# w_down in a decode block's feed-forward stage: two half transfers become one of four rows per partition, and its products move ahead of the gates

## The chip, the cores and the metric

The kernel runs on one core of one Trainium2 chip. The metric is the device time of one execution in microseconds. Before the change the median of three runs is 599.42 us (598.52 to 600.30).

## What is computed

The reference is one transformer block for a single token (batch 1, one row of D = 1024), its output and the gradients with respect to ten of its inputs: eleven outputs, the first of them the block's own. The block modulates a layer norm by a condition vector `c`, attends to the last 4096 of 65536 cached keys and values (32 query heads, 4 key heads), and then runs a gated feed-forward part:

```
h   = layernorm(x) * (1 + cb) + sb
g   = h @ w_gate          # (1024, 3584)
u   = h @ w_up            # (1024, 3584)
hh  = sigmoid(g) * u
ffn = hh @ w_down         # (3584, 1024)
x   = x + gb * ffn
```

The feed-forward part's gradients that matter here are, with `dffn = grad_out * gb` a row of 1024:

- d(w_down) = hh (outer product) dffn, 3584 x 1024;
- dhh = w_down @ dffn, a vector of 3584;
- du = dhh * sigmoid(g), dg = dhh * hh * (1 - sigmoid(g)), together `dug`;
- d(w_gate) and d(w_up) = h (outer product) dg and du;
- dh = w_gate @ dg + w_up @ du.

The gradients of the two caches have the caches' full shape, 65536 rows for each of 4 heads. All rows outside the window of 4096 are zero, and the kernel has to write them: this is the largest part of its traffic.

## The kernel before, in words

The kernel is one program with an order written out by hand. Each engine runs its own instructions in that order, and waits where an operand or a buffer isn't ready. DMAs are issued from two queues: SP (SyncE) and POOL (GpSimd). All of them are carried by the same 16 DMA engines. In the profile the SP queue's packets are q1 and POOL's are q0. Each queue's issuing engine is in order: an issue that waits holds all behind it.

**Fills.** The zero rows are written by 1 MB DMAs of a tile `zeros`, issued by `zero(n)` (line 169 in the profile) on POOL. How many stand at which place is fixed by lists at the top of the file (`Z_N`, `Z_B`, `Z_FOLD`, `Z_FFN`, `Z_END`). They serve as filler that keeps the DMA engines at work beside the loads and stores. In the feed-forward loop five blocks have three of them each, `(1, 0, 0, 2)`, the sixth has five and the last has four.

**Feed-forward stage.** F = 3584 is cut into NB = 7 blocks q of 512. For each block:

- w_gate and w_up arrive as 8 tiles j of 128 rows, in a double buffer `ug_v` (index q % 2). `load_ug(q, j0, 4)` issues two 512 KB loads, `store_ug` two 512 KB stores of the gradients, which take the place of the weights in the same buffer. Both are on POOL.
- w_down arrives in `wd_v`, one buffer of 8 KB per partition for all blocks, as two halves s of 256 rows. A half has two rows per partition. `load_wd(q, s)` and `store_wd(q, s)` are on SP. The gradient of w_down overwrites the weights in place, so the load of block q+1 has to wait until the store of block q has landed.
- `front(q)` (line 954, PE): 64 small products of `ug_v` with h2, giving g and u in PSUM. Which of the 512 features lies in which partition and column is set by w_down's row layout: feature 256*(i//2) + 2*p + i%2 stands in partition p, column i. PE reads `ug_v` with a step of 2 for this.
- `gates(q)` (lines 959 and 960, ACT): two sigmoids. `hh_ops(q)` (DVE): hh in bf16 and in f32, and hh*(1-sigmoid).
- `ffn_mm(q, s)` (line 971, PE): 16 products of a half of w_down with hh.
- `wd_ttr(q, s)` (DVE, the helper `ttr` at line 210, writes into `junk`): two multiply-and-sum instructions over 1024 columns, dhh = w_down . dffn. `b1k` is dffn broadcast to all partitions.
- `wd_outer(q, s)` (DVE, the helper at line 206): two outer products that overwrite the half of w_down by its gradient, then `store_wd`.
- `dug_part(q)`: two small DVE products, 8 PE transposes (line 990) and one ACT copy (line 991) that broadcast dug into `dug_b`, 1024 columns.
- The loop over j = 0..7: `ttr` of the tile with `dug_b` (DVE, line 210, in place), then an outer product into the tile, on ACT for j < 5 (line 241) and on DVE for the rest. Gate and up tiles 0 to 3 are stored after j = 3, 4 to 7 after j = 7.

`side()` takes one unit of unrelated work from a list: eight PE transposes (line 837) and an ACT copy (line 838).

For block q+1 the order before is: front, gates, one side unit, hh_ops, ffn_mm and two ttr of the first half, load of half the gate and up tiles of block q+2, two outer products and the store of the first half, side unit, the same for the second half with dug_part ahead of its outer products, the second half of the gate and up loads, the fills, and both w_down loads of block q+2.

After this stage come further gradients (attention, the projections, the modulation), and large stores to the end.

The functions that the diff touches:

Of the kernel before, what the change touches and what calls it, by code (L numbers as in the profile page):

```python
# [22 lines left out]
FB = 512  # L23
NB = F // FB
# [34 lines left out]
def kernel(  # L59
# [26 lines left out]
    nc = tc.nc  # L86
# [13 lines left out]
    def ar(off, size):  # L100
        return arena[:, int(off * KIB):int((off + size) * KIB)]
# [86 lines left out]
    def new_tp(name="tp"):  # L188
        p, tag = next_pool()
        return p.tile([P, 1024], BF16, name=name, tag=tag)  # L190
# [4 lines left out]
    def mulv(out, a, b):  # L195
        return tt(out, a, b, ALU.mult)

    def addv(out, a, b):
        return tt(out, a, b, ALU.add)

    def cp(out, a):
        return nc.vector.tensor_copy(out=out, in_=a)  # L202
# [6 lines left out]
    def ttr(out, w, b, acc):  # L209
        return nc.vector.tensor_tensor_reduce(out=out, in0=w, in1=b, scale=1.0, scalar=0.0,  # L210
                                              op0=ALU.mult, op1=ALU.add, accum_out=acc)
# [31 lines left out]
    def outer_dve(out, col, b):  # L243
        return ts(out, b, col, ALU.mult)
# [96 lines left out]
    def mod_tiles(ps, tiles, ts_, first, last=KD - 1):  # L341
        for t in ts_:
            for k in range(KD):
                nc.tensor.matmul(ps[:, k:k + 1], lhsT=tiles[t][:, k * P:(k + 1) * P],
                                 rhs=cs_bf[:, t:t + 1], start=(first and t == ts_[0] and k == 0), stop=(t == last),
                                 skip_group_check=True)
# [98 lines left out]
    def side(n=1):  # L445
        for _ in range(n):
            if jobs:
                jobs.pop(0)()
# [61 lines left out]
    for tb in range(4):  # L510
# [3 lines left out]
        tp = new_tp("tp_pT")  # L514
# [111 lines left out]
    for g in range(G):  # L626
        nbank = bank_pair("n_ps", g)
        for t_ in range(KT):
            s = g * KT + t_
# [52 lines left out]
    def bch(n=1):  # L682
        for _ in range(n):
            if not bq:
                return
            p, i, u = bq.pop(0)
            if i == 0:
                bbank[p] = bank_pair("b_ps", p)
            for a in range(4):
                h = 4 * u + a  # L690
                for k in range(2):
                    mm = nc.tensor.matmul(bbank[p][k][:, :], lhsT=a4[:, p, h, :], rhs=wo_t[u][:, a, k * 512:(k + 1) * 512],  # L692
                                          start=(i == 0 and a == 0), stop=(i == 7 and a == 3))
            zero(Z_B[nbq - 1 - len(bq)], recent(mm, 3))
            if i == 7:
                for k in range(2):
                    o = B_t[p][:, k * 512:(k + 1) * 512]
                    if k == 0 or p == NBP - 1:
                        nc.scalar.copy(out=o, in_=bbank[p][k][:, :])
                    else:  # L700
                        cp(o, bbank[p][k][:, :])
# [81 lines left out]
    def park(p, pl, tag):  # L783
        BT_ps[p] = pl.tile([P, D], BF16, name="BT_ps", tag=tag)
        for i in range(KD):
            nc.tensor.transpose(BT_ps[p][:, i * P:(i + 1) * P], B_t[p][:, i * P:(i + 1) * P], ident_bf[:, :])
# [58 lines left out]
    ug_v = arena[:, 16 * KIB:48 * KIB].rearrange("p (h q j k f) -> p q h j k f", h=2, q=2, j=4, k=2)  # L845
    wd_v = ar(152, 8).rearrange("p (i d) -> p i d", i=4)

    def wd_dram(t, q, s):
        return t[q * FB + s * 256:q * FB + s * 256 + 256, :].rearrange("(p j) d -> p j d", j=2)

    def load_wd(q, s):
        nc.sync.dma_start(out=wd_v[:, 2 * s:2 * s + 2, :], in_=wd_dram(B_w_down, q, s))

    def store_wd(q, s):
        nc.sync.dma_start(out=wd_dram(out_8, q, s), in_=wd_v[:, 2 * s:2 * s + 2, :])

    def ug_part(view, q, j0, n):
        return view[:, j0:j0 + n, q * FB:(q + 1) * FB]
# [8 lines left out]
    def store_ug(q, j0, n):  # L867
        for k, view in ((0, dwu_view), (1, dwg_view)):
            nc.gpsimd.dma_start(out=ug_part(view, q, j0, n), in_=ug_tile(q, k, j0, n))  # L869
# [23 lines left out]
    load_ug(0, 4, 4)  # L893
    park(2, pna, "na")
    park(3, pna, "na")
    load_wd(0, 0)
    bch(2)
    tr_unit(B_t[6], ar(56, 2))()
    cp(scr, B_t[4])
    B_t[4] = scr  # L900
    load_wd(0, 1)
    mod_tiles(md_ps, sb_t, range(4, 8), False)
    cp(sb_, md_ps[:, 0:KD])
    mulv(h2, ln2, cb1)
# [32 lines left out]
    dug_b = scr  # L937
# [10 lines left out]
    def front(q):  # L948
        gu = gu_t[q % 2]
        for col, k in ((4, 0), (0, 1)):  # L950
            for i in range(4):
                f0 = 256 * (i // 2) + i % 2
                for j in range(KD):
                    nc.tensor.matmul(gu[:, col + i:col + i + 1], lhsT=ug_v[:, q % 2, j // 4, j % 4, k, f0:f0 + 255:2],  # L954
                                     rhs=h2_bf[:, j:j + 1], start=(j == 0), stop=(j == KD - 1))

    def gates(q):
        r, gu = small[q % 2], gu_t[q % 2]
        nc.scalar.activation(out=r["sg"], in_=gu[:, 0:4], func=ACT.Sigmoid)
        nc.scalar.activation(out=r["om"], in_=gu[:, 0:4], func=ACT.Sigmoid, scale=-1.0)  # L960

    def hh_ops(q):
        r, up = small[q % 2], gu_t[q % 2][:, 4:8]
        mulv(r["hh_bf"], r["sg"], up)
        mulv(r["hh"], r["sg"], up)
        mulv(r["hom"], r["hh"], r["om"])

    def ffn_mm(q, s):
        for i in (2 * s, 2 * s + 1):
            for k in range(KD):  # L970
                nc.tensor.matmul(ffn_ps[:, k:k + 1], lhsT=wd_v[:, i, k * P:(k + 1) * P],
                                 rhs=small[q % 2]["hh_bf"][:, i:i + 1], start=(i == 0 and k == 0),
                                 stop=(i == 3), skip_group_check=True)

    def wd_ttr(q, s):
        for i in (2 * s, 2 * s + 1):
            ttr(junk, wd_v[:, i, :], b1k, small[q % 2]["dhh"][:, i:i + 1])

    def wd_outer(q, s):
        for i in (2 * s, 2 * s + 1):  # L980
            outer_dve(wd_v[:, i, :], small[q % 2]["hh"][:, i:i + 1], b1k)
        store_wd(q, s)

    def dug_part(q):
        r = small[q % 2]
        mulv(r["dug_bf"][:, 0:4], r["dhh"], r["sg"])
        mulv(r["dug_bf"][:, 4:8], r["dhh"], r["hom"])
        tp = new_tp("tp_dug")
        for i in range(8):
            nc.tensor.transpose(tp[:, i * P:(i + 1) * P], r["dug_bf"][:, i:i + 1].broadcast_to([P, P]), ident_bf[:, :])  # L990
        nc.scalar.copy(out=dug_b.rearrange("p (s f j) -> p s f j", s=4, j=2),  # L991
                       in_=tp.rearrange("p (s j f) -> p s f j", s=4, j=2))

    jobs.append(tr_unit(B_t[7]))
    for h in range(HQ):
# [3 lines left out]
    def unpark(p):  # L999
        nc.scalar.copy(out=B_home[p], in_=BT_ps[p][:, :])  # L1000

    front(0)
    gates(0)
    hh_ops(0)
    ffn_mm(0, 0)
    wd_ttr(0, 0)
    side(2)
    wd_outer(0, 0)
    ffn_mm(0, 1)
    wd_ttr(0, 1)  # L1010
    side(1)
    dug_part(0)
    wd_outer(0, 1)
    zero(Z_FOLD[2])
    load_wd(1, 0)
    load_wd(1, 1)
    for q in range(NB):
        z = Z_FFN[q]
        more = q + 1 < NB
        for j in range(KD):  # L1020
            w = ug_v[:, q % 2, j // 4, j % 4, :, :].rearrange("p k f -> p (k f)")
            ttr(w, w, dug_b, dh2acc[:, q * KD + j:q * KD + j + 1])
            if not more and j in (3, 5, 6):
                unpark({3: 2, 5: 0, 6: 4}[j])
            (outer_act if j < 5 else outer_dve)(w, h2[:, j:j + 1], dug_b)
            if more and 0 < j < 5:
                side()
            if j == 0:
                if q == 0:
                    cp(ffn, ffn_ps)  # L1030
                else:
                    addv(ffn, ffn, ffn_ps)
            if j == 3:
                store_ug(q, 0, 4)
                zero(z[0])
        store_ug(q, 4, 4)
        zero(z[1])
        if more:
            front(q + 1)
            gates(q + 1)  # L1040
            side()
            hh_ops(q + 1)
            ffn_mm(q + 1, 0)
            wd_ttr(q + 1, 0)
            if q + 2 < NB:
                load_ug(q + 2, 0, 4)
            wd_outer(q + 1, 0)
            zero(z[2])
            side()
            ffn_mm(q + 1, 1)  # L1050
            wd_ttr(q + 1, 1)
            side()
            dug_part(q + 1)
            wd_outer(q + 1, 1)
            if q + 2 < NB:
                load_ug(q + 2, 4, 4)
            zero(z[3])
            if q + 2 < NB:
                load_wd(q + 2, 0)
                load_wd(q + 2, 1)  # L1060
        else:
            zero(z[2] + z[3])
    assert not jobs
# [269 lines left out]
```

## Time and profile before

| | |
|---|---|
| median of 3 runs | 599.42 us |
| the profiled execution, time | 598.03 us |
| its span | 596.2 us |
| PE, DVE, ACT, POOL busy | 69%, 57%, 45%, 27% of the span |
| moved by DMA | 246.63 MB, mean 414 GB/s |
| software queue (POOL) | 217.60 MB, packets took 95.1% of 16 engines |
| hardware queue (SP) | 28.32 MB, 13.1% |
| feed-forward stage, first block's loop to the last block's loop | 324.4 to 464.0 us of the span |
| DMA rate in that stage | 407 GB/s |

The span is the time from the first to the last record of the profile. Rows of a chain or a timeline give the start in us from the span's start, the duration in us, and then the instruction: engine, line, tile. A row `DMA out_dram<-arena` in the chain is the time from a DMA's issue until what waited for its landing could go on. In a timeline, what stands in square brackets is how long the engine was idle before, and what ended it. The queue shares can sum to over 100%, as packets of the two queues overlap on an engine. The clock that was granted to PE in the feed-forward stage is 0.50.

### The profile page before, as it was taken

What the parts mean: (1) busy time and instruction counts of PE and PEld (TensorE: products, weight loads), DVE (VectorE), ACT (ScalarE), POOL (GpSimd) and SP (SyncE); (2) the same over time, 40 slices, a digit from 0 to 9 for tenths busy, and PEclk for the clock granted to TensorE, in tenths of its full rate; (3) what the DMA queues carried; (4) which work ended last, traced back from release to release, by engine and by line L of the source; (5) the groups of instructions that cost most, each with busy time, mean ns of one, the idle gap of its engine ahead of it and who ended that gap; (6) DMA issues with size and microseconds to landing.
All of it is one profiled execution on the core that took longest, in us unless ns stands there. A gap on an engine that the chain in (4) does not pass through costs nothing.

```text
span 596.2 us, 11043 instructions
## 1 busy us (share of the span) xinstructions
PE 409.2 (69%) x4587; PEld 275.6 (46%) x4612; DVE 337.7 (57%) x641; ACT 266.0 (45%) x408; POOL 159.4 (27%) x253
## 2 busy tenths in 40 slices
PE   3997688999999989999975436445445086774220
PEld 3995334334344545546654425434334066574220
DVE  3654499999511010070007587896787887858360
ACT  2589514567211014212224565773765835883110
POOL 3113123222222122222222224433423263223100
PEclk9999699999999999999995555555555586855555
DMA  8999999999999999999999999999999999999997
GB/s 348 421 417 420 413 425 417 426 425 424 429 420 424 421 430 422 423 423 423 422 399 412 420 387 414 404 405 409 403 410 408 420 420 413 422 423 426 424 426 326
DMA packets 45026, 246.63 MB, mean 414 GB/s; under 512 B 5085, under 2 KB 5085, under 8 KB 24544
## 3 DMA queue, kind: packets, MB, share of 16 engines
q0 software_dynamic: 37536, 217.60, 95.1%
q1 hardware_dynamic: 7392, 28.32, 13.1%
q8 instruction: 36, 0.59, 0.4%
q14 instruction: 14, 0.11, 0.0%
q10 hardware_dynamic: 48, 0.01, 0.0%
HBM read 60.30 MB, written 185.60 MB: 412 GB/s over the span
## 4 chain that ended last, share of the span: by engine, by line
DMA 38%; PE 32%; DVE 16%; ACT 5%; issue 4%; POOL 0%; DVEq 0%; ACTq 0%; POOLq 0%; SPq 0%
DMA out_dram<-arena 18%; PE b_ps L692 10%; DMA out_dram<-zeros 9%; PE n_ps L637 6%; DMA arena<-in_B_w_gate_dram 6%; DVE arena L206 5%; DMA arena<-in_B_w_down_dram 4%; DVE arena L193 4%; DVE junk L210 2%; PE t_ps L599 2%; DVE arena L210 2%; PE tp_wq L454 2%; PE w_ps L395 2%; PE tp_side L837 1%; PE tp_k L435 1%
## 5 line engine op out<-in xcount | busy, mean ns | idle before, releaser
L692 PE MATMUL b_ps<-arena 128*128 128x512 bf16 x494 | 113.4, 379 | 1.0 <-issue 0.2
L169 POOL DMA_DIRECT2D out_dram<-zeros x114 | 62.3, 548 | 178.7 <-DMA out_dram<-zeros 57.4
L837 PE MATMUL tp_side<-ident_bf,arena 128*128 128x128 bf16 x432 | 51.7, 300 | 48.1 <-ACT arena L838 41.2
L193 DVE TENSOR_TENSOR arena<-arena 128x2048 bf16<-128x2048 bf16 x64 | 76.5, 1223 | 2.3 <-PE n_ps L637 0.3
L692 PEld LDWEIGHTS <-arena 128*128 128x128 bf16 x512 | 48.7, 98 | 55.9 <-issue 2.9
L838 ACT COPY arena<-tp_side 128x1024 bf16<-128x1024 bf16 x54 | 54.0, 1012 | 42.7 <-PE tp_side L837 41.8
L210 DVE CUSTOM_DVE_ANT_0 arena<-arena,scr 128x1024 bf16<-128x1024 bf16 x56 | 66.2, 1220 | 9.9 <-ACT scr L991 9.9
L637 PE MATMUL n_ps<-arena 128*128 128x512 bf16 x249 | 65.1, 378 | 6.9 <-DVE arena L193 5.0
L837 PEld LDWEIGHTS <-arena 128*128 128x128 bf16 x432 | 43.4, 139 | 53.0 <-issue 52.6
L241 ACT ACTIVATE arena<-scr,h 128x1024 bf16<-128x1024 bf16 x35 | 40.1, 1149 | 9.6 <-DVE dh2acc L210 7.8
L637 PEld LDWEIGHTS <-arena 128*128 128x128 bf16 x256 | 24.6, 97 | 41.6 <-issue 16.2
L1162 ACT ACTIVATE arena<-ps_kv 128x512 bf16<-128x512 f32 x48 | 26.1, 680 | 30.4 <-PE ps_kv L1158 30.0
L202 DVE CAST arena<-b_ps 128x512 bf16<-128x512 f32 x6 | 4.2, 692 | 61.6 <-PE b_ps L692 61.6
L210 DVE CUSTOM_DVE_ANT_0 junk<-arena,b1k 128x1024 bf16<-128x1024 bf16 x28 | 34.2, 1222 | 6.8 <-DMA arena<-in_B_w_down_dram 6.3
L1158 PE MATMUL ps_kv<-junk,arena 8*128 8x128 bf16 x256 | 27.1, 303 | 13.9 <-DVE arena L206 12.6
L601 ACT CAST arena<-t_ps 128x512 bf16<-128x512 f32 x56 | 30.1, 589 | 12.1 <-PE t_ps L599 12.1
L869 POOL DMA_DIRECT2D out_dram<-arena x28 | 21.5, 772 | 42.6 <-ACT arena L241 32.1
L1158 PEld LDWEIGHTS <-arena 8*128 8x128 bf16 x256 | 25.2, 140 | 15.6 <-issue 15.6
L456 ACT COPY arena<-tp_wq 128x1024 bf16<-128x1024 bf16 x23 | 21.7, 1041 | 7.9 <-PE tp_wq L454 7.9
L865 POOL DMA_DIRECT2D arena<-in_B_w_up_dram x14 | 10.6, 755 | 48.1 <-DMA out_dram<-arena 24.8
L954 PE MATMUL fg<-h_bf,arena 128*128 128x1 bf16 x448 | 14.7, 166 | 11.5 <-DMA arena<-in_B_w_gate_dram 8.7
L206 DVE TENSOR_SCALAR arena<-arena,cs_col 128x4096 bf16<-128x4096 bf16 (+1 forms) x16 | 16.1, 1020 | 10.3 <-DMA out_dram<-arena 10.2
(302 smaller groups left out, 639.5 us busy)
## 6 DMA issues: line engine op xcount, KB each, us to landing
out_dram<-zeros POOLq DMA_DIRECT2D x114, 1024.0 KB, 16.2
out_dram<-arena POOLq DMA_DIRECT2D x27, 1024.0 KB, 19.0
out_dram<-arena POOLq DMA_DIRECT2D x30, 512.0 KB, 11.9
out_dram<-arena SPq DMA_DIRECT2D x20, 512.0 KB, 9.2
arena<-in_A_wq_dram POOLq DMA_DIRECT2D x8, 1024.0 KB, 20.7
arena<-in_A_wo_dram POOLq DMA_DIRECT2D x8, 1024.0 KB, 12.5
arena<-in_w_mod_dram POOLq DMA_DIRECT2D x7, 1024.0 KB, 18.2
arena<-in_B_w_down_dram SPq DMA_DIRECT2D x14, 512.0 KB, 8.9
```

The lines of the kernel that those rows point to most:

```text
L169: ins = nc.gpsimd.dma_start(out=region.bitcast(FP32), in_=zeros[:, :])
L193: return nc.vector.tensor_tensor(out=out, in0=a, in1=b, op=op)
L206: return nc.vector.tensor_scalar(out=out, in0=a, scalar1=s1, scalar2=None, op0=op0)
L210: return nc.vector.tensor_tensor_reduce(out=out, in0=w, in1=b, scale=1.0, scalar=0.0, op0=ALU.mult, op1=ALU.add, accum_out=acc)
L241: return nc.scalar.activation(out=out, in_=b, func=ACT.Copy, scale=col)
L601: nc.scalar.copy(out=o, in_=ps)
L637: mm = nc.tensor.matmul(nbank[k][:, :], lhsT=k_nat[:, g, t_ * DH:(t_ + 1) * DH], rhs=vp[:, t_ % 2, 4 * k:4 * k + 4, :].rearrange("p h d -> ...
L692: mm = nc.tensor.matmul(bbank[p][k][:, :], lhsT=a4[:, p, h, :], rhs=wo_t[u][:, a, k * 512:(k + 1) * 512], start=(i == 0 and a == 0), stop= ...
L837: nc.tensor.transpose(tp[:, i * P:(i + 1) * P], blk[:, i * P:(i + 1) * P], ident_bf[:, :])
L838: nc.scalar.copy(out=blk if dst is None else dst, in_=tp[:, :])
L1158: nc.tensor.matmul(ps[:, t4 * DH:(t4 + 1) * DH], lhsT=rows[32 * g:32 * g + HG, t_ * P:(t_ + 1) * P], rhs=hd[32 * g:32 * g + HG, :], start= ...
L1162: nc.scalar.activation(out=o, in_=ps[:, :], func=ACT.Copy, scale=float(scale))
```

## The change

One w_down transfer per block, 1 MB with four rows per partition (8 KB that are contiguous in DRAM), takes the place of two of 512 KB with two rows per partition. This sets a new layout: feature 4*p + i stands in partition p, column i, so `front` reads its weights with a step of 4, and `dug_part` sorts four groups in place of two.

In the order of the program, the four ttr of block q+1 stand right behind the loop over j of block q, then two side units, then front, gates, hh_ops, dug_part and ffn_mm of block q+1. The four outer products of block q, its store of w_down's gradient and the load of w_down for block q+1 stand inside the loop over j of block q, behind the outer product of j = 0. The places of the fills and of the gate and up DMAs in POOL's order stay the same.

```diff
@@ -845,14 +845,14 @@
     ug_v = arena[:, 16 * KIB:48 * KIB].rearrange("p (h q j k f) -> p q h j k f", h=2, q=2, j=4, k=2)
     wd_v = ar(152, 8).rearrange("p (i d) -> p i d", i=4)
 
-    def wd_dram(t, q, s):
-        return t[q * FB + s * 256:q * FB + s * 256 + 256, :].rearrange("(p j) d -> p j d", j=2)
-
-    def load_wd(q, s):
-        nc.sync.dma_start(out=wd_v[:, 2 * s:2 * s + 2, :], in_=wd_dram(B_w_down, q, s))
-
-    def store_wd(q, s):
-        nc.sync.dma_start(out=wd_dram(out_8, q, s), in_=wd_v[:, 2 * s:2 * s + 2, :])
+    def wd_dram(t, q):
+        return t[q * FB:(q + 1) * FB, :].rearrange("(p i) d -> p i d", i=4)
+
+    def load_wd(q):
+        nc.sync.dma_start(out=wd_v, in_=wd_dram(B_w_down, q))
+
+    def store_wd(q):
+        nc.sync.dma_start(out=wd_dram(out_8, q), in_=wd_v)
 
     def ug_part(view, q, j0, n):
         return view[:, j0:j0 + n, q * FB:(q + 1) * FB]
@@ -893,12 +893,11 @@
     load_ug(0, 4, 4)
     park(2, pna, "na")
     park(3, pna, "na")
-    load_wd(0, 0)
     bch(2)
     tr_unit(B_t[6], ar(56, 2))()
     cp(scr, B_t[4])
     B_t[4] = scr
-    load_wd(0, 1)
+    load_wd(0)
     mod_tiles(md_ps, sb_t, range(4, 8), False)
     cp(sb_, md_ps[:, 0:KD])
     mulv(h2, ln2, cb1)
@@ -949,9 +948,8 @@
         gu = gu_t[q % 2]
         for col, k in ((4, 0), (0, 1)):
             for i in range(4):
-                f0 = 256 * (i // 2) + i % 2
                 for j in range(KD):
-                    nc.tensor.matmul(gu[:, col + i:col + i + 1], lhsT=ug_v[:, q % 2, j // 4, j % 4, k, f0:f0 + 255:2],
+                    nc.tensor.matmul(gu[:, col + i:col + i + 1], lhsT=ug_v[:, q % 2, j // 4, j % 4, k, i:i + 509:4],
                                      rhs=h2_bf[:, j:j + 1], start=(j == 0), stop=(j == KD - 1))
 
     def gates(q):
@@ -965,21 +963,21 @@
         mulv(r["hh"], r["sg"], up)
         mulv(r["hom"], r["hh"], r["om"])
 
-    def ffn_mm(q, s):
-        for i in (2 * s, 2 * s + 1):
+    def ffn_mm(q):
+        for i in range(4):
             for k in range(KD):
                 nc.tensor.matmul(ffn_ps[:, k:k + 1], lhsT=wd_v[:, i, k * P:(k + 1) * P],
                                  rhs=small[q % 2]["hh_bf"][:, i:i + 1], start=(i == 0 and k == 0),
                                  stop=(i == 3), skip_group_check=True)
 
-    def wd_ttr(q, s):
-        for i in (2 * s, 2 * s + 1):
+    def wd_ttr(q):
+        for i in range(4):
             ttr(junk, wd_v[:, i, :], b1k, small[q % 2]["dhh"][:, i:i + 1])
 
-    def wd_outer(q, s):
-        for i in (2 * s, 2 * s + 1):
+    def wd_outer(q):
+        for i in range(4):
             outer_dve(wd_v[:, i, :], small[q % 2]["hh"][:, i:i + 1], b1k)
-        store_wd(q, s)
+        store_wd(q)
 
     def dug_part(q):
         r = small[q % 2]
@@ -988,8 +986,8 @@
         tp = new_tp("tp_dug")
         for i in range(8):
             nc.tensor.transpose(tp[:, i * P:(i + 1) * P], r["dug_bf"][:, i:i + 1].broadcast_to([P, P]), ident_bf[:, :])
-        nc.scalar.copy(out=dug_b.rearrange("p (s f j) -> p s f j", s=4, j=2),
-                       in_=tp.rearrange("p (s j f) -> p s f j", s=4, j=2))
+        nc.scalar.copy(out=dug_b.rearrange("p (k f i) -> p k f i", k=2, i=4),
+                       in_=tp.rearrange("p (k i f) -> p k f i", k=2, i=4))
 
     jobs.append(tr_unit(B_t[7]))
     for h in range(HQ):
@@ -999,21 +997,15 @@
     def unpark(p):
         nc.scalar.copy(out=B_home[p], in_=BT_ps[p][:, :])
 
+    wd_ttr(0)
+    side(2)
     front(0)
     gates(0)
     hh_ops(0)
-    ffn_mm(0, 0)
-    wd_ttr(0, 0)
-    side(2)
-    wd_outer(0, 0)
-    ffn_mm(0, 1)
-    wd_ttr(0, 1)
+    dug_part(0)
+    ffn_mm(0)
     side(1)
-    dug_part(0)
-    wd_outer(0, 1)
     zero(Z_FOLD[2])
-    load_wd(1, 0)
-    load_wd(1, 1)
     for q in range(NB):
         z = Z_FFN[q]
         more = q + 1 < NB
@@ -1026,6 +1018,9 @@
             if more and 0 < j < 5:
                 side()
             if j == 0:
+                wd_outer(q)
+                if more:
+                    load_wd(q + 1)
                 if q == 0:
                     cp(ffn, ffn_ps)
                 else:
@@ -1036,28 +1031,20 @@
         store_ug(q, 4, 4)
         zero(z[1])
         if more:
+            wd_ttr(q + 1)
+            side(2)
             front(q + 1)
             gates(q + 1)
+            hh_ops(q + 1)
+            dug_part(q + 1)
+            ffn_mm(q + 1)
             side()
-            hh_ops(q + 1)
-            ffn_mm(q + 1, 0)
-            wd_ttr(q + 1, 0)
             if q + 2 < NB:
                 load_ug(q + 2, 0, 4)
-            wd_outer(q + 1, 0)
             zero(z[2])
-            side()
-            ffn_mm(q + 1, 1)
-            wd_ttr(q + 1, 1)
-            side()
-            dug_part(q + 1)
-            wd_outer(q + 1, 1)
             if q + 2 < NB:
                 load_ug(q + 2, 4, 4)
             zero(z[3])
-            if q + 2 < NB:
-                load_wd(q + 2, 0)
-                load_wd(q + 2, 1)
         else:
             zero(z[2] + z[3])
     assert not jobs
```

## Prediction

> **What bounds the kernel now.** I read the page's 40 slices first, then the windows of the feed-forward stage, then the chain of waits there, then the DMA answers by queue, then DVE's timeline. Times are from the one profiled execution: 598.03 us, span 596.2. The median of the runs is 599.42, 1.39 above it.
>
> ```profile
> DMA  8999999999999999999999999999999999999997
> GB/s 348 421 417 420 413 425 417 426 425 424 429 420 424 421 430 422 423 423 423 422 399 412 420 387 414 404 405 409 403 410 408 420 420 413 422 423 426 424 426 326
> ```
>
> The DMA engines are busy in every slice, at some 424 GB/s, while PE is busy 69% and DVE 57%: the kernel is bound by bytes. The slices that fall short (numbers 20 to 30) are the feed-forward stage. In windows, it moves 407 GB/s from 324.4 to 464.0 us, and 422 from there to 575.
>
> ```profile
> 318.77 8.67 DMA out_dram<-arena
> 327.51 14.06 DMA arena<-in_B_w_down_dram
> 341.60 1.23 DVE junk L210
> 342.86 1.23 DVE junk L210
> ...
> 345.16 8.01 DMA out_dram<-arena
> 353.22 10.38 DMA arena<-in_B_w_down_dram
> 363.62 1.23 DVE junk L210
> ...
> 379.73 19.77 DMA out_dram<-arena x2
> ...
> 400.04 7.86 DMA arena<-in_B_w_gate_dram
> 407.95 1.73 PE fg L954 x59
> ```
>
> This is the chain of waits there (start, us, what). In two blocks out of seven it is the round trip of w_down's only buffer: store of the gradient, then the next block's load, then its products (ttr, L210 into junk). Later it is the same round trip of the gate and up tiles. So this stage stands close to two latencies as well as to the DMA engines. I call J(q) the start of block q's first DVE product over gate and up; from DVE's timeline J is 324.38, 350.44, 371.75, 393.28, 418.45, 440.95, 463.96. A block lasts 23.3 us on average. The bytes of a block (56.82 MB between the first and last J, a sixth is 9.47) need 22.3 us at 424 GB/s, so 1 us a block is lost today.
>
> **What the change does to w_down's round trip.** Before, a half is stored right after its two products and two outer products, ahead of J; the halves run staggered, and the load of a half needs only its own store. From a half's load landing to its store's issue there are two ttr and two outer products: 341.60 to 345.16, 3.6 us. All else of the block lies beside the trip. After, the one buffer is one tile: the outer products of block q stand behind the first product of the gate and up loop, then come store, load, and all four ttr of block q+1, and only behind those hh, dug, the broadcast and J(q+1). The compute between a landing and the next store's issue, on DVE's only queue:
>
> ```profile
> 385.17 1.22 DVE L210 CUSTOM_DVE_ANT_0 junk<-arena,b1k 128x1024 bf16<-128x1024 bf16 x1
> ...
> 387.58 0.88 DVE L206 TENSOR_SCALAR arena<-b1k,hh 128x1024 bf16<-128x1024 bf16 x2
> ...
> 388.38 1.22 DVE L210 CUSTOM_DVE_ANT_0 junk<-arena,b1k 128x1024 bf16<-128x1024 bf16 x1
> ...
> 391.06 0.87 DVE L206 TENSOR_SCALAR arena<-b1k,hh 128x1024 bf16<-128x1024 bf16 x2
> 393.28 1.23 DVE L210 CUSTOM_DVE_ANT_0 arena<-arena,scr 128x1024 bf16<-128x1024 bf16 x1 [1.35 <-ACT scr L991]
> ```
>
> - four ttr: two take 385.17 to 387.58, 2.4, so 4.8 us;
> - three hh products and two dug products: 0.34 and 0.16 in the same timeline, 0.5;
> - dug to J (eight transposes, ACT's copy, semaphores): 391.06 to 393.28, 2.2;
> - first ttr of the loop 1.15 and four outer products, 0.80 a pair: 2.75.
>
> Sum 10.25. With R for the round trip of store and load, a block lasts 10.25 + R. The rest of the loop (seven ttr and three outer products, 10 us on DVE) hides in R; so do front, the gates and ffn_mm, unless gate and up come late. Their chain (last outer, store, load, front, J) spans two blocks; the four ttr and two of the outers between front and J leave it (about 5.5 us less), and the four outers inside the loop enter it (1.6 more), so it gets looser. No queue but SP's gets a new order that counts: POOL's instructions keep theirs, and SP has only w_down here. What is queued behind the new wait of ttr on the load: on DVE the whole next block; on PE the dug transposes, then ffn_mm and the side transposes; on ACT the dug copy; on POOL the next block's stores and fills, and that is what lets the DMA engines run dry.
>
> **How long R is.** The trace of before has no 1 MB w_down transfer. These are the nearest rows: the half stores (L855), the half loads (L852), and SP's 1 MB stores at the kernel's end, also 8 KB per partition.
>
> ```profile
> DMA to landing us min/median/max: 8.1/8.4/9.7
> ```
> ```profile
> DMA to landing us min/median/max: 6.6/8.9/14.1
> ```
> ```profile
> out_dram<-arena SPq DMA_DIRECT2D x4, 1024.0 KB, 9.9
> ```
>
> A second 512 KB at 424 GB/s adds 1.24 to each. From below: 8.1 + 6.6 + 2.5 = 17.2. From above: 10.2 (SP's 1 MB store issued at 554.97 in the tail, from its line's landings) + 14.1 + 1.24 = 25.5. Below even the first stands a case with free DMA engines, which no row shows; its effect is the second rival. I take 17.2, the low end, because a longer block leaves the engines idle some of the time: 9.47 MB in 27.4 us is 345 GB/s. For the first trip I take the first one of today, 8.67 + 14.06 = 22.7, since the same run of fills stands beside it.
>
> A page disagrees: the Trainium skill, DMA: Bandwidth & Descriptors, section "Anatomy of one DMA — SWDGE (gpsimd) path", fits one DMA by 2.0 us plus bytes at 436 GB/s, and its section "Rules for kernel authors" asks for 1 MiB per DMA. By that estimate R is 8.8 and a block 19.1 us, which would be no bound at all and the change a gain. The shortest half store here already takes 8.1 us, beside other queues' traffic, so I go by the rows.
>
> **The sum.** J(0) comes sooner: b1k is written at 312.02, plus 4.8, 0.5 and 2.2 gives 319.5 (front ends at 314.8, or some 1.5 later behind the two side units, still in time). J(1) = 319.5 + 10.25 + 22.7 = 352.5. J(6) = 352.5 + 5 x 27.45 = 489.7, against 463.96: 25.7 later. The last block's outers now stand inside the loop: +1.6. What follows is bound by bytes (422 GB/s), so the delay passes to the end, less what was still queued at the last J: POOL issues no DMA from 460.2 to 470.99 today and the engines stay busy, some 9 us of queue that will be worked off by then, of which some 6 come back as a gap before the first store of that block: -3. In all +24.3, 622.3 on the profiled 598.03; on the median, 623.7. I say 623.
>
> **Edits I cost at nothing.** Half as many w_down DMAs of 8 KB rows save at most SP's issue time, off the path. Front's weights are read with step 4 in place of 2: 448 loads, 104 ns each now; if they doubled, 64 x 0.1 = 6.7 us a block would still lie beside R, and on the path without that cover. ACT's copy of dug now gathers from four places in place of two; today it takes 1012 ns, just as the contiguous copies of L838. It is on the path: between 0 and +1.0 a block, I take 0.
> By the Trainium skill (Advanced Engine Details and Errata, section "PSUM Cachelines") a pattern that is not contiguous in PSUM slows matmuls; the page prices no ACT copy, and the equal 1012 ns speak against any cost for one.
>
> **Rivals.**
> 1. *R stays as long as under today's load* (20 to 22.7, as the first trips showed): J(6) = 352.5 + 5 x 30.25..32.95 = 503.8 to 517.3, less 463.96 and less the same 1.4, +38 to +52: 638 to 651 on the median. For it: the 14.06 us load ran while four fills were under way, and fills stay beside the trip. Against it: the engines would be idle a quarter of the time (9.47 MB in 30.3 us is 313 GB/s), and a transfer that meets less traffic should land sooner.
> 2. *Faster: emptier engines and one large transfer make R short.* The point that decides is 319.5 + 6 x (10.25 + R) = 463.96, R = 13.8. Below it the bytes bound again, at best all blocks at 22.3 us: 6 x 1.0 = 5.8 saved, 593.6. For it: dug follows front 5 us sooner, which takes gate and up off the path. Against it: stores and loads of R lie beside a block's other 7.4 MB; the shortest rows alone sum to 14.7 for a half.
> 3. *Hidden: within 0.3%*, 597.6 to 601.2. DVE's last computation ends near 576 and DMA runs on to 596; if the fills cover the trip, nothing moves. Against it: the fills stand in POOL's order, three a block, behind stores that wait for the loop; the tail is bytes and takes up no delay.
>
> **How the numbers follow.** Forecast 0.69, rival 1 0.14, rival 2 0.10, rival 3 0.07. A difference of 0.3% is about what a measurement of this kernel can tell. Faster 0.10, same 0.07, slower 0.83. With R from 13.8 to 21.3 in the steady blocks the time is 607 to 644, plus the uncertain copy; with part of rival 3 the range is 601 to 645.
>
> **What would show it.** Right: a chain in which w_down's store, load and four ttr recur in every block; J some 27 apart; DVE idle before ttr for 5 us or more a block; the feed-forward slices well under 400 GB/s. Wrong: store and load of 1 MB landing within 6.9 us each; or front's gate load still last in the chain; or blocks of 30 and more (rival 1). If the dug copy is over 1012 ns, or J(0) is not near 319.5, those terms are off.

## Result and profile after

The changed kernel takes 618.83 us (median of 4 runs, 617.43 to 619.51), against 599.08 for the kernel before (median of 4). The ratio on record, estimated over the runs of both, is 1.0313, 95% interval 1.0282 to 1.0343; the two medians divide to 1.0330, which lies within it. The forecast was 623. Of all executions below, one of E2's four fell in a slower state (616.48 us) and is left out of E2's numbers. The profiled execution took 619.25 us with a span of 617.4, 21.2 more than the profiled execution of before.

The page's DMA rows of the changed kernel, in 40 equal slices:

```profile
DMA  9999999999999999999999989999998999999997
GB/s 352 419 418 422 413 426 397 422 427 426 421 424 423 425 426 421 422 426 424 401 410 415 377 307 358 416 343 332 385 345 305 425 415 405 409 423 425 425 425 297
```

Up to slice 22 and from slice 32 on the rates are close to those of before. In slices 23 to 31, which lie in the feed-forward stage, they fall to between 305 and 416 GB/s. The bytes are the same 246.63 MB, so the lost time is there. The starts J of the seven blocks, from DVE's timeline, are 324.35, 358.43, 379.17, 411.23, 431.97, 464.70 and 485.45. The blocks therefore last 34.1, 20.7, 32.1, 20.7, 32.7 and 20.8 us: long and short ones take turns. The windows of the first four blocks show the same (columns: window, its length, busy time of PE, PEld, DVE, ACT and POOL, granted clock, DMA share, GB/s):

```profile
324.40:358.40 34.00, 11.02 (x160) 9.89 (x160) 17.75 (x37) 13.56 (x15) 7.70 (x11) 0.50 1.07 400
358.40:379.20 20.80, 11.04 (x161) 9.92 (x161) 17.98 (x38) 13.57 (x15) 6.64 (x9) 0.50 0.87 314
379.20:411.10 31.90, 11.04 (x160) 9.92 (x160) 17.76 (x37) 13.47 (x15) 9.82 (x14) 0.50 1.05 386
411.10:432.00 20.90, 11.06 (x161) 9.93 (x161) 17.81 (x38) 13.66 (x16) 5.83 (x8) 0.50 0.88 323
```

DVE does the same 18 us of work in each. What differs is the wait of the first product. SP's timeline shows the trip of w_down (L855 store, L852 load; the load is issued when the store has landed):

```profile
361.29 0.34 SPq L855 DMA_DIRECT2D out_dram<-arena  x1
365.20 0.33 SPq L852 DMA_DIRECT2D arena<-in_B_w_down_dram  x1
382.02 0.34 SPq L855 DMA_DIRECT2D out_dram<-arena  x1
393.70 0.33 SPq L852 DMA_DIRECT2D arena<-in_B_w_down_dram  x1
```

The store lands in 3.9 us in the short block and in 11.7 in the long one. The rows of DVE that end the two trips:

```profile
371.00 1.21 DVE L210 CUSTOM_DVE_ANT_0 junk<-arena,b1k 128x1024 bf16<-128x1024 bf16 x1
...
403.56 1.23 DVE L210 CUSTOM_DVE_ANT_0 junk<-arena,b1k 128x1024 bf16<-128x1024 bf16 x1 [11.92 <-DMA arena<-in_B_w_down_dram]
```

In the short block DVE comes to the product straight from the loop, so the trip is hidden and the block lasts as long as DVE's own order takes, 20.7. In the long block DVE stands still for 11.92 us, and the queues run dry behind it; the next trip then meets engines with little to do. Three windows show this, columns as above: the store of 361.29 meets a DMA share of 0.29 and its load one of 0.32, while the share is 1.03 for as long as the store of 382.02 takes.

```profile
360.00:362.00 2.00, 1.01 (x8) 0.85 (x8) 2.00 (x6) 1.56 (x2) 0.00 (x0) 0.50 0.29 94
364.00:366.00 2.00, 1.01 (x8) 0.85 (x8) 2.00 (x5) 1.95 (x3) 0.00 (x0) 0.50 0.32 131
382.00:394.00 12.00, 4.57 (x38) 3.76 (x37) 9.53 (x18) 9.54 (x10) 3.58 (x5) 0.50 1.03 392
```

The waits of DVE on w_down's load in this stage sum this up (total, times, longest), first in the changed kernel, between 324 and 490, then in the kernel before:

```profile
DVE junk L210 <- DMA arena<-in_B_w_down_dram: 38.3, 3, 13.9
...
DVE junk L210 <- DMA arena<-in_B_w_down_dram: 6.3, 3, 5.0
```

### The profile page after: what moved, and what is told of

It is laid out like the page before. It is cut to its first block, busy times and chain, and to the rows that moved or that the text cites. A ratio compares the mean times of both kernels' runs of the same rounds, so it can differ in the third digit from the quotient of the medians.

```text
span 617.4 us, 11002 instructions
## 1 busy us (share of the span) xinstructions
PE 413.6 (67%) x4587; PEld 279.9 (45%) x4612; DVE 336.8 (55%) x641; ACT 265.5 (43%) x408; POOL 158.6 (26%) x253
## 2 busy tenths in 40 slices
DMA packets 43011, 246.63 MB, mean 399 GB/s; under 512 B 4862, under 2 KB 4862, under 8 KB 20737
## 5 line engine op out<-in xcount | busy, mean ns | idle before, releaser
L210 DVE CUSTOM_DVE_ANT_0 arena<-arena,scr 128x1024 bf16<-128x1024 bf16 x56 | 66.2, 1220 | 14.7 <-ACT scr L989 10.5
L838 ACT COPY arena<-tp_side 128x1024 bf16<-128x1024 bf16 x54 | 54.0, 1012 | 40.3 <-PE tp_side L837 39.4
L210 DVE CUSTOM_DVE_ANT_0 junk<-arena,b1k 128x1024 bf16<-128x1024 bf16 x28 | 34.3, 1224 | 39.1 <-DMA arena<-in_B_w_down_dram 38.3
L869 POOL DMA_DIRECT2D out_dram<-arena x28 | 21.5, 771 | 89.6 <-ACT arena L241 79.8
L988 PE MATMUL tp_dug<-ident_bf,dug_bf 128*128 128x128 bf16 x56 | 7.2, 311 | 42.6 <-DVE dug_bf L193 42.6
L1145 PEld LDWEIGHTS <-arena 8*128 8x128 bf16 x256 | 25.3, 140 | 17.5 <-issue 17.5
L989 ACT COPY scr<-tp_dug 128x1024 bf16<-128x1024 bf16 x7 | 7.1, 1012 | 48.5 <-issue 48.5
L456 ACT COPY arena<-tp_wq 128x1024 bf16<-128x1024 bf16 x23 | 21.8, 1032 | 8.3 <-PE tp_wq L454 8.3
L988 PEld LDWEIGHTS <-dug_bf 128*128 128x128 bf16 x56 | 5.4, 141 | 43.2 <-DVE dug_bf L193 43.2
```

The costliest lines, as they stand in the source:

```text
L838: nc.scalar.copy(out=blk if dst is None else dst, in_=tp[:, :])
L1145: nc.tensor.matmul(ps[:, t4 * DH:(t4 + 1) * DH], lhsT=rows[32 * g:32 * g + HG, t_ * P:(t_ + 1) * P], rhs=hd[32 * g:32 * g + HG, :], start= ...
```

## Experiments

Theory A is the forecast's: the order is at fault, since one buffer's round trip has all of the next block's products, gates and broadcast behind it. Theory B blames the single 1 MB transfer, theory C the new order's own work. Each ratio is to the kernel before on the same chip.

**E1, new order with the old halves.** The helpers of before (two halves, two rows per partition) in the changed kernel's order.

```diff
             if j == 0:
+                for s in range(2):
+                    wd_outer(q, s)
+                if more:
+                    for s in range(2):
+                        load_wd(q + 1, s)
...
+            wd_ttr(q + 1, 0)
+            wd_ttr(q + 1, 1)
+            side(2)
             front(q + 1)
```

> The new order with the old transfers: two halves of two rows per partition, as before, but all four products ahead of front, and the four outer products, both stores and both loads inside the loop behind j = 0. Theory A (the order is at fault: the one buffer's round trip now has 10.25 us of products, gates and broadcast behind it): slow like the changed kernel, 612 to 621; somewhat better than it, as the first half is stored 0.8 us sooner and its products can begin before the second half lands. Theory B (the single 1 MB transfer is at fault, for the halves no longer run staggered): near the kernel before, 597 to 604.

Measured: 617.11 us, ratio 1.0286 (1.0267 to 1.0306). The order alone costs 17.7 us, nearly all of it. Its blocks last 22.4 to 31.2 us, without the strict turns, and DVE's waits on w_down sum to 32.0 us.

**E2, one transfer in the old order.**

```diff
             front(q + 1)
             gates(q + 1)
             side()
             hh_ops(q + 1)
-            ffn_mm(q + 1, 0)
-            wd_ttr(q + 1, 0)
...
+            ffn_mm(q + 1)
+            wd_ttr(q + 1)
...
-            wd_outer(q + 1, 0)
...
             dug_part(q + 1)
-            wd_outer(q + 1, 1)
+            wd_outer(q + 1)
...
-                load_wd(q + 2, 0)
-                load_wd(q + 2, 1)
+                load_wd(q + 2)
```

> The new transfer with the old order: one 1 MB transfer of four rows per partition, but front, gates and hh first, then the four products, dug, and the four outer products, store and load ahead of the loop. From landing to the next store's issue there are four ttr, the dug products and four outer products, 4.8 + 0.2 + 1.7 = 6.7 us in place of 10.25. Theory A: a block lasts 6.7 plus a round trip of about 17, 23 to 24 us, so 598 to 607. Theory B: slow like the changed kernel, 613 to 621.

Measured: 607.87 us (three executions), ratio 1.0130 (1.0109 to 1.0151), just above theory A's range. Blocks after the first last 23.3 to 24.5 us. DVE waits for w_down's load in all six of them, 29.1 us in total. In the middle of the stage the chain of waits is nothing but w_down's trip and its compute:

```profile
379.42 9.29 DMA out_dram<-arena
388.77 6.97 DMA arena<-in_B_w_down_dram
395.77 1.23 DVE junk L210
...
401.07 1.60 DVE arena L206 x4
402.69 6.29 DMA out_dram<-arena
409.03 10.78 DMA arena<-in_B_w_down_dram
419.83 1.23 DVE junk L210
```

Trips of 16.3 and 17.1 us, with 6.9 us from landing to the next store's issue, where the kernel before has 3.6 for a half. So the single transfer costs too, though less: without the halves' stagger the products of one half can't run while the other half is on its trip. The two parts alone cost 17.7 and 8.4 us and both together 19.8. They don't add; both lengthen the same loop, which is the likely reason. All five of E2's trips after the first last 16.3 to 17.5 us: where the blocks are even, the forecast's 17.2 was right.

**E3, outer products ahead of the loop.**

```diff
+            ffn_mm(q + 1)
             dug_part(q + 1)
-            ffn_mm(q + 1)
+            wd_outer(q + 1)
+            if q + 2 < NB:
+                load_wd(q + 2)
...
             if j == 0:
-                wd_outer(q)
-                if more:
-                    load_wd(q + 1)
```

> The changed kernel with one part moved: ffn_mm ahead of dug_part, and the four outer products, the store and the next load right behind the dug products, so that they fill DVE's 2.1 us of waiting for dug's broadcast instead of standing behind the first ttr of the loop. Landing to store is 4.8 + 0.5 + about 2 in place of 10.25. Theory A: each long block loses about 3 us, six trips some 10 to 18 us in all, 601 to 610. Theory B: no more than 3 us better than the changed kernel, 615 to 620.

Measured: 608.32 us, ratio 1.0141 (1.0101 to 1.0181). From landing to the next store's issue there are now some 7.5 us in place of 10.5 (397.06 to 404.60). Taking these 3 us out gives back a little over half of the loss, which fits A and not B. Blocks are 32.1, 27.5, then 23.2 to 24.7; the strict turns are gone.

**E4, a second buffer.**

```diff
-    wd_v = ar(152, 8).rearrange("p (i d) -> p i d", i=4)
+    wd_2 = [ar(o, 8).rearrange("p (i d) -> p i d", i=4) for o in (152, 128)]
...
     wm_sec(5, 5, 1, 60, nc.sync)
+    load_wd(1)
...
                 wd_outer(q)
-                if more:
-                    load_wd(q + 1)
+                if q + 2 < NB:
+                    load_wd(q + 2)
```

> The changed kernel with a second w_down buffer, laid over the transposed modulation weights that the last matvec needs, so the condition vector's gradient is computed from overwritten weights; all instructions run. The load of block q+2 waits for the store of block q and has a whole block of time. Theory A (the round trip through one buffer is all of the loss): the wait of the products on the load is gone, a block is bound by bytes or by gate and up, 22.3 to 23.3 us, so 592 to 600. Theory C (the loss is the new order's own, by DVE or by the fills' place in POOL's order): 608 or more. Theory B expects a gain too, but keeps 1 MB transfers slow: 600 to 610.

Measured: 599.77 us (10 runs), ratio 1.0007 (0.9994 to 1.0020). With the new order, the new layout and the 1 MB transfers all in place, the loss is gone once the trip is off the path. That settles A against C, and against a cost of the 1 MB transfer as such. But it isn't faster than before either, although DVE never waits for w_down, its blocks last 21.8 us on average in place of 23.3, and its last block starts at 459.5 and not 464.0. What follows takes that much longer, 137.1 us from there to the span's end in place of 132.2. The window of the stage, from its first J to its last:

```profile
328.80:459.50 130.70, 66.97 (x960) 59.92 (x960) 107.72 (x222) 81.37 (x90) 44.79 (x64) 0.50 1.07 404
```

404 GB/s, as in the kernel before (407), and in both the DMA engines are busy 90% or more in each of 40 slices of that window. So the shortfall of this stage against 424 GB/s is not the trip's: the trip had no time to give. What keeps the rate at 404 to 407 was not tested.

**E5, no fills between the blocks.** `Z_FFN = [(0, 0, 0, 0)] * 7`; the 24 fills are issued at the end.

> The changed kernel without fills between its blocks: all 24 zero fills of the feed-forward loop are issued at the end of the kernel instead (all bytes are still written). Its long blocks (32 to 34 us) and short ones (21 us) should part by what the DMA queues hold while w_down is on its trip. Theory A1 (the fills that stand in POOL's queue stretch the trip): the trip is 9 to 12 us in every block, all blocks last 20.7 to 23 us, the stage's DMA rate falls to some 300 GB/s, and the whole time grows to 615 to 632, since the fills are no longer hidden there. Theory A2 (the gate and up transfers alone stretch it): long and short blocks still alternate, 28 us or more and 21.

Measured, one run: 650.92 us. The total missed its range: right behind the stage, slices 29 and 30 of its page fell to 136 and 269 GB/s, and the 25 MB of fills came only at the end. What the run was for came out: after the first block (33.4 us, four fills from ahead of the stage still under way) the blocks last 20.7, 20.7, 22.4, 20.7 and 20.7. The windows of the first block and of the other five:

```profile
320.80:354.20 33.40, 11.04 (x160) 9.92 (x160) 17.79 (x38) 13.56 (x15) 6.66 (x10) 0.50 1.01 369
354.20:459.50 105.30, 55.20 (x800) 49.59 (x800) 89.09 (x185) 67.80 (x75) 27.18 (x36) 0.50 0.80 280
```

At a DMA share of 0.80 the same trip through one buffer costs next to nothing: DVE waits for w_down 3.2 us in these five blocks together. It is the load on the DMA engines that makes the trip long.

**E6 and E10, the fills elsewhere in POOL's order**: `(1, 2, 0, 0)` and `(0, 0, 0, 3)` in the first five blocks in place of `(1, 0, 0, 2)`.

> The changed kernel with the two last fills of each of the first five blocks moved in POOL's order from behind the gate and up loads to ahead of them, behind the gradients' stores. The next block's w_down store then meets gate and up loads in place of two fills. Theory A1: the long blocks lose up to 5 us each, 606 to 614. Theory A2, or that only the amount queued counts: no change, 616 to 621.

> The changed kernel with all three fills of each of the first five blocks behind the gate and up loads, where it has one between the stores and two there. With none there the time was 613.3, with two 618.8. Theory A1 (what POOL has queued right before w_down's store stretches the trip): 620 to 625, long blocks of 34 us or more. If only the amount queued in a block counts: 617 to 620.

Measured: 613.33 us, ratio 1.0214 (1.0184 to 1.0243), and 615.07 us, ratio 1.0263 (1.0236 to 1.0289). E6 alone would have spoken for A1, that what stands queued right before w_down's store is what counts. E10 speaks against it, and lies outside both of its ranges: more fills there made the kernel not slower but, if anything, faster than the changed one (1.0282 to 1.0343). Both keep long and short blocks (E6 29.0 to 29.7 and 20.7 to 21.0, E10 30.5 to 32.2 and 20.8 to 22.3, after a first of 38.1 and 34.3). E5 shows that without the stage's fills there are no turns. The fills alone don't make them, since E1, E2 and E3 have the same fills and no strict turns; how the fills' place acts stays open.

**E7, the first w_down load behind the modulation loads.**

```diff
-    load_wd(0)
...
     wm_sec(5, 5, 1, 60, nc.sync)
+    load_wd(0)
```

> The changed kernel with the first w_down load behind the two modulation loads on SP, not ahead of them. The forecast had the first block's loop start at 319.5; it starts at 324.4, as dffn's broadcast came 4 us late. If the cause is the 1 MB load ahead of those loads in SP's queue: the loop starts at 319 to 321.5 and the time falls by 2 to 5 us, 613 to 617. If not: 324 and no change.

Measured: 617.23 us, ratio 1.0281 (1.0249 to 1.0314), not told apart from the changed kernel. J(0) is 323.8: b1k came 2.4 us sooner, and then the first product waited 2.48 us for w_down. E5, E6 and E10, which issue the very same program up to there as the changed kernel, start at 320.7 or 320.8. So most of the miss of J(0) is a difference between executions, not SP's order.

**E8, all three**: E3's order, E6's fills, E7's load.

> The outer products ahead of the loop, the fills ahead of the gate and up loads, and the first w_down load behind the modulation loads, all in one: can the single transfer with its products ahead of the gates be brought to the time of the kernel before? The outer products ahead of the loop gave 608.3. If the other two add what they are expected to: 597 to 604. If the trip is still the bound: 605 to 609.

Measured: 613.89 us, ratio 1.0219 (1.0169 to 1.0269): outside both ranges and slower than E3 alone by the medians, though the two intervals just touch. The turns are back (28.9 to 29.8 and 20.4 to 22.1 us after the first). The moves don't add. Why E3's outer products with the old place of the fills keep the blocks even and with the new one don't was not settled.

**E9, the layout alone**: the helpers of before, in the old order, on four rows per partition; a half takes two of the four.

```diff
-        return t[q * FB + s * 256:q * FB + s * 256 + 256, :].rearrange("(p j) d -> p j d", j=2)
+        return t[q * FB:(q + 1) * FB, :].rearrange("(p i) d -> p i d", i=4)[:, 2 * s:2 * s + 2, :]
...
```

> The kernel before with the new layout alone: four rows per partition, front's weights with step 4, dug gathered from four places, but still two transfers of 512 KB (two of the four rows of each partition, 4 KB runs) and the old order. The forecast costs the layout at nothing: 597 to 601, the dug copy at 1012 ns. If the weights' step or the copy cost something on the path: up to 7 us a part, 602 to 612.

Measured: 599.80 us (10 runs), ratio 0.9996 (0.9984 to 1.0008). In the old order the layout costs nothing that these runs can tell.

## Why the prediction was right

The cause and the sign held: w_down's trip through its one buffer is what costs, and E4 gives all of it back. The forecast was +23.6 on the median, measured +19.8. What did not hold is that the trip binds every block alike; that the total came so close is in part luck. By its steps, with the profiles of before and after:

- *Compute from landing to the next store's issue*, 10.25. Measured from 350.77 (first product) to 361.29 (store issued): 10.5. Right.
- *J(0) = 319.5.* It is 324.35 here, 320.7 to 323.8 in E5, E6, E7 and E10: 1.2 to 4.9 late, and different from one execution to the next.
- *First trip 22.7, J(1) - J(0) = 33.0.* Store issued at 327.20, product at 350.77: 23.6, and the block lasts 34.1. Right.
- *R = 17.2 in each steady block, 27.45 a block.* This is the term that was mis-sized, and its shape was wrong too. The five blocks last 25.4 us on average, and no block lasts 27. R comes in two kinds: about 21.5 to 22.2 when the queues are full (382.02 to 403.56, and the like), which is close to rival 1's 20 to 22.7, and 3.9 for the store and some 5 for the load when they are not. Then DVE's own order sets the block, 20.7; the forecast let the loop's DVE work hide in R and had no block that it bounds. So rivals 1 and 2 each describe the trip of every second block. As a size, 17.2 fits E2's even loop (16.3 to 17.5); what failed was to carry it into a loop that swings. "A longer block leaves the engines idle some of the time" was right, but it was taken as a mean, while the loop swings: a long block drains the queues, a short one fills them.
- *After the last J*: forecast -1.4 (outers +1.6, queue -3), measured 131.95 us from J(6) to the span's end against 132.24 before, -0.3.
- The sum: J(6) 21.5 later (forecast 25.7), less 0.3, is the span's 21.2. The terms' errors partly cancel: +6 by J(1), -10 by the five steady blocks. This is the luck in the total: 4.9 of the +6 is J(0), of which three executions of the same program up to that point show only 1.2 to 1.3.
- *Edits at nothing*: the layout, the weights' step and the dug copy cost nothing that E9 can tell; the copy still takes 1012 ns.
- *Rival 2's price* was wrong. It held that below R = 13.8 the blocks could give back up to 5.8 us, from "1 us a block is lost today". E4 takes the wait on the trip away altogether; its blocks do get shorter, 21.8 us, but the total gives back nothing. So the time lost in the stage before, 407 GB/s in place of 424, did not come from waiting for w_down.
- *What would show it*: the waits on w_down and most of the slices under 400 came, but the waits only in every second block (13.95, 11.92 and 12.40 us), and J some 27 apart did not. The chain that ended last goes back only to 482.7 us and says nothing of the blocks. Two of the signs of being wrong came as well, by turns: blocks of 30 and more, and a store and a load of 1 MB within 6.9 us each.

The fit in the Trainium skill, DMA: Bandwidth & Descriptors, section "Anatomy of one DMA — SWDGE (gpsimd) path", gives 4.4 us for 1 MiB. It is fitted for DMAs issued by GpSimd, while w_down goes over SP; the stores of 3.9 and loads of 4.8 us in the short blocks are near it all the same. The fit has no term for what else is queued; the 11.7 and 9.9 us of the long block from 379.17 on are what this kernel pays with the queues full.

## What to carry to other kernels

When one buffer is stored and refilled in a loop, count all the compute between a load's landing and the next store's issue: where the trip binds, it adds in full to the round trip, and moving work "ahead" in the program can put it into that loop. Take the round trip's length from the load that the DMA engines will carry at that time, and expect it to swing with the loop if waits drain the queues. Where the DMA engines are busy all the time, as in the kernel before, taking the wait away gave nothing back (E4), while a longer chain cost up to 19.8 us.

## What the runs showed that was not expected

A 1 MB transfer over SP takes 3.9 us (store) or 4.8 us (load) from issue to landing in the changed kernel's short blocks, and up to 14.15 and 9.9 us in its long ones: 3.6 times and twice as long. E5 shows that this goes by what else the DMA engines carry. That such a loop settles into turns of 20.7 and some 32 us instead of a mean was not expected. Reading the front's weights with step 4 in place of 2 raises the median of PE's weight loads from 104 to 118 ns (E9, 448 of them), with no effect on the time.
